# Attention on raw tokens, two taps per product, and smaller moves in a four-layer convolution and attention kernel

## The chip, the core and the metric

The kernel runs on one core of a Trainium2 chip. The metric is device microseconds of one execution; a time given for a kernel is the median of several. The profile comes from one further execution, taken by the hardware profiler. Its engines are PE (matrix multiplication, with PEld for its weight loads), DVE (vector), ACT (scalar), POOL (used here for fills alone) and SP, which issues the DMA transfers.

## The reference

A sequence of 2048 tokens with 512 features passes four layers, each with a residual. Layers 1 and 3 are a long convolution (a state-space kernel K of 128 modes per feature, multiplied with the input in a Fourier transform of length 4096; Kf and Uf below are the spectra); layers 2 and 4 are local attention with 32 heads of 16 features, in which a token looks at itself and at the seven tokens that lie 2, 4, ..., 14 before it. Both kinds get layer-normalized tokens, and the same weights serve both layers of a kind. In the code below q, k and v are the three parts of x @ wqkv, and kg and vg are k and v gathered at idx.

```python
def _layernorm(x, axis=-1, eps=1e-5):
    m = jnp.mean(x, axis=axis, keepdims=True)
    v = jnp.var(x, axis=axis, keepdims=True)
    return (x - m) / jnp.sqrt(v + eps)
...
def _A_ref(u, A_re, A_im, B_re, B_im, C_re, C_im, log_dt, Dskip):
    ...
    P = jnp.exp(logdA[:, :, None] * l[None, None, :])
    K = jnp.einsum("dn,dnl,dn->dl", Cc, P, dB).real
    ...
    Yf = Uf * Kf[None, :, :, :]
    ...
def _B_ref(x, wqkv, wo):
    ...
    idx = pos[:, None] - off[None, :]
    mask = idx >= 0
    ...
    logits = jnp.einsum("bhsd,bhswd->bhsw", q, kg) * scale
    logits = jnp.where(mask[None, None, :, :], logits, -1e9)
    attn = _softmax(logits, axis=-1)
    o = jnp.einsum("bhsw,bhswd->bhsd", attn, vg)
    return (lambda x, *d: x.transpose(*d))(o, 0, 2, 1, 3).reshape(B, S, D) @ wo

x = A_u
x = x + _A_ref(_layernorm(x, axis=-1), ...)
x = x + _B_ref(_layernorm(x, axis=-1), B_wqkv, B_wo)
x = x + _A_ref(_layernorm(x, axis=-1), ...)
x = x + _B_ref(_layernorm(x, axis=-1), B_wqkv, B_wo)
```

## The kernel before

The tokens `X` stay in on-chip memory as 128 partitions by 16 rows of 512 features; token p*16+j is row j of partition p. So a tap that lies 2w tokens back is row j-2w of the same partition, or of the partition before it, for which `shift` and a like transfer of kT copy the last rows one partition down.

Order. Each operation is registered with `Plan.op` with its engine, a planned duration in microseconds and what it needs; `Plan.either` registers several ways to do one step (on ACT or DVE, by PE or DMA). `Plan.run` then issues them in an order that is written out by hand in `ORDERS`, five strings of operation numbers, which also settles which way is taken. Each engine works through its share of that order, waiting where an input isn't there. The strings are in turn: preparation, kernel tables and first convolution, attention 1, convolution 2, attention 2.

Preparation and tables (`prepare`, `kernel_and_first_conv`). The convolution's kernel is built from tables of powers on DVE. Their factors, the multipliers A and B, come from casts on ACT (L556); A is stored twice side by side so that a factor meets pairs of elements. The table products (L391, L399, L456) are summed on PE (L431, L469).

Convolution. Spectra come from PE and are multiplied by the kernel's spectrum in two DVE products of 1024 elements each, `pa` and `pb` (L931, L932 in the first layer, L1176, L1177 in the second), which are joined with a sum and a difference, transformed back on PE, evacuated to `VT` (L959, L1205; its last index runs over 128 features), and brought into X by final matmuls (L981, L1222) and an evacuation (L985, L1227).

Attention (`b_layer`). It opens with 15 matmuls that nobody reads (L1271). For each quarter of four rows, `start` does statistics on DVE (L153; parts of them lie in the convolution's tail), a square root on ACT (L166), a reciprocal (L178), the normalization into `xn` (L193 on DVE, L1288 on ACT), and the transposes into `xnT`, by DMA (L1294) or PE (L1299). `proj` makes q and k (L1324, evacuated at L1329), `values` makes v (L1344, evacuated into `VX` at L1349). `logits` multiplies q with k for each of eight taps on DVE (L1375), 40 products a layer; PE sums the 16 features of a head with the 32-column matrix `bones` (L1385). The logits are copied, transposed and evacuated to `L` (L1400, L1408, L1411), the first partition's missing taps are filled by POOL (L1451), and a tree of maxima (L1430), a subtraction (L1473), Exp on ACT (L1474), a sum on PE (L1468), a reciprocal on DVE (L1456) and a multiplication (L1476) make the softmax. `pv` multiplies each tap's v with its weight on DVE (L1487) and PE sums the taps (L1503, L1508). The result is copied and turned (L1523, L1528) and multiplied by wo (`out`, L1560), and X is added by PE or DVE (L1543).

The attention's weights are loaded before the first convolution ends (L128 to L132, at 189.5 to 193 us).

Of the kernel before, what the change touches and what calls it, by code (L numbers as in the profile page):

```python
# [11 lines left out]
ALU = mybir.AluOpType  # L12
# [29 lines left out]
TWO_PI = 2.0 * np.pi  # L42

# [79 lines left out]
def load_b_weights(nc, const, wqkv, wo):  # L123
    wqk = const.tile([128, 4, 1024], BF, name="wqk")
    wo_t = const.tile([128, 4, 512], BF, name="wo_t")
    wv = const.tile([128, 4, 512], BF, name="wv")
    wsrc = wqkv.rearrange("(t p) f -> p t f", p=128)
    nc.sync.dma_start(wqk[:], wsrc[:, :, 0:1024])  # L128
    nc.sync.dma_start(wv[:], wsrc[:, :, 1024:1536])
    for ft in range(4):  # L130
        src = wo[ft * 128:(ft + 1) * 128, :].rearrange("(h d) o -> d h o", d=DH)
        nc.sync.dma_start(wo_t[:, ft, :], src)  # L132
    VX = const.tile([128, 2, NV + NJ, 256], BF, name="VX")
    nc.gpsimd.memset(VX[0:1, :, 0:NV], 0.0)
    return dict(wqk=wqk, wv=wv, wo=wo_t), VX


class LnStats:


    def __init__(self, nc, pool, parts, nm, eps, tag="", st=None):
        self.nc, self.parts, self.eps = nc, parts, eps
        p, t = st or (pool, "ln_st" + tag)
        self.st = p.tile([128, NJ, len(parts), 6], F32, name="ln_st_" + nm, tag=t)
        self.mv = pool.tile([128, NJ, 2], F32, name="ln_mv_" + nm, tag="ln_mv" + tag)
        self.den = pool.tile([128, NJ], BF, name="ln_den_" + nm, tag="ln_den" + tag)
        self.rstd = pool.tile([128, NJ], F32, name="ln_rstd_" + nm, tag="ln_rstd" + tag)
        self.nb = pool.tile([128, NJ], F32, name="ln_nb_" + nm, tag="ln_nb" + tag)
# [6 lines left out]
    def finish(self, j0, j1):  # L155
        self.gathered(j0, j1)
        self.root(j0, j1)
        self.scale(j0, j1)

# [12 lines left out]
    def root_of_squares(self, j0, j1):  # L172
        js = slice(j0, j1)
        self.nc.scalar.activation(self.den[:, js], self.sq[:, js], ACT.Sqrt, bias=self.eps[:, 0:1], scale=1.0 / D)

    def invert(self, j0, j1):
        js = slice(j0, j1)
        self.nc.vector.reciprocal(self.rstd[:, js], self.den[:, js])  # L178
# [4 lines left out]

    def scale(self, j0, j1):
        self.invert(j0, j1)
        self.offset(j0, j1)
# [9 lines left out]
def load_params(nc, pp, prm):  # L196
# [1533 lines left out]
```

## The time and profile before

| | |
|---|---|
| median of 3 runs | 498.18 us (497.74 to 498.95) |
| profiled execution, first to last instruction | 495.2 us; its own device time was not taken, the median lies 3.0 above the span |
| tables and first convolution | 0 to 204.9 us |
| attention 1 | 204.9 to 320.6 us (its last vector work ends at 325.65, beside convolution 2) |
| convolution 2 | 320.6 to 377.3 us |
| attention 2 | 377.3 to 495.2 us |
| busy | PE 411.3, DVE 457.7, ACT 349.0, POOL 13.0 us |
| granted clock of PE | 0.979 |

A stage here begins when the last part of X of the stage before is written. Times in the prediction's profile lines are microseconds from the span's start; a group's line gives the line of code, engine, operation, destination and sources, shapes, count, then busy time in all, mean nanoseconds of one, and the idle time before it with what ended it.

### The profile page before, as it was taken

To read this page: it belongs to the slowest core of one execution; us is meant where nothing else is said; L and a number is where in the kernel's file an instruction comes from. 1 tells how busy PE (TensorE), PEld (TensorE's weight loads), DVE (VectorE), ACT (ScalarE), POOL (GpSimd) and SP (SyncE) were. 2 spreads that over 40 slices of the span, in tenths; PEclk is the share of its full clock that TensorE was granted. 3 is DMA by queue.
4 is the path that set the end of the run, shared out by engine and by line. 5 is a ranking of instruction groups with operands and counts; after the bars stand their busy time and mean duration, and the time that the engine had idled before them with its cause. 6 is when DMAs were issued, how large, how long until landed. Compare 5 with 4: busy or idle time off the path is not lost.

```text
span 495.2 us, 12551 instructions
## 1 busy us (share of the span) xinstructions
PE 411.3 (83%) x5262; PEld 244.4 (49%) x5279; DVE 457.7 (92%) x774; ACT 349.0 (70%) x522; POOL 13.0 (3%) x63
## 2 busy tenths in 40 slices
PE   2602397988898989789999889979998999997996
PEld 1501262665575667543355434565675434563343
DVE  6999999999999998859899999988999689999996
ACT  6999986988778769764664359878997657643340
POOL 0000000000000004000000000000000000000000
PEclk9999698999999999999999989989999999999999
DMA  8930025448556846280031232559901500222217
GB/s 263 197 160 0 1 68 130 81 115 192 114 114 162 152 109 195 68 126 32 18 91 38 58 65 42 165 125 210 182 4 21 112 29 31 77 61 58 42 29 205
DMA packets 101596, 48.81 MB, mean 99 GB/s; under 512 B 86443, under 2 KB 93868, under 8 KB 101284
## 3 DMA queue, kind: packets, MB, share of 16 engines
q1 hardware_dynamic: 101108, 47.62, 41.6%
q8 instruction: 41, 0.67, 0.6%
q10 hardware_dynamic: 432, 0.39, 0.2%
q14 instruction: 15, 0.12, 0.1%
HBM read 15.78 MB, written 8.13 MB: 48 GB/s over the span
## 4 chain that ended last, share of the span: by engine, by line
PE 35%; DVE 12%; DMA 8%; ACT 7%; issue 5%; SPq 1%; POOL 0%; DVEq 0%; ACTq 0%
PE ps_qk L1324 7%; PE po L1503 4%; DVE prod L1487 4%; PE ps_v L1344 4%; PE ps_o L1560 3%; DVE prod L1375 3%; DMA VX<-VX 2%; PE Lp L1385 2%; DMA zt<-Z 2%; PE ps_y L1222 1%; PE vp L1196 1%; PE vp L1200 1%; DMA xnT<-xn 1%; ACT L L1474 1%; ACT Z L845 1%
## 5 line engine op out<-in xcount | busy, mean ns | idle before, releaser
L1375 DVE TENSOR_TENSOR prod<-qT,kT 128x2048 bf16<-128x2048 bf16 (+1 forms) x80 | 76.9, 1006 | 12.6 <-ACT kT L1329 9.9
L1487 DVE TENSOR_TENSOR prod<-VX,L 128x2048 bf16<-128x2048 bf16 (+2 forms) x96 | 77.3, 862 | 1.3 <-DMA VX<-VX 1.0
L1324 PE MATMUL ps_qk<-xnT,wqk 128*128 128x512 bf16 x256 | 61.4, 380 | 1.5 <-DMA xnT<-xn 1.3
L1503 PE MATMUL po<-prod,sb_ident 128*128 128x512 bf16 x216 | 53.5, 379 | 4.8 <-DVE prod L1487 3.7
L1324 PEld LDWEIGHTS <-wqk 128*128 128x128 bf16 x256 | 22.8, 97 | 31.9 <-issue 9.7
L1503 PEld LDWEIGHTS <-sb_ident 128*128 128x128 bf16 x224 | 21.2, 98 | 31.3 <-DVE prod L1487 5.1
L1344 PE MATMUL ps_v<-wv,xnT 128*128 128x256 bf16 x256 | 32.1, 273 | 1.9 <-ACT xnT L1302 1.4
L431 PE MATMUL ps_sum<-Ttab,sb_ident 128*128 128x512 bf16 x36 | 15.1, 420 | 22.2 <-DVE Ttab L391 21.4
L1349 ACT CAST VX<-ps_v 128x512 bf16<-128x512 f32 x32 | 18.6, 587 | 19.8 <-PE ps_v L1344 19.7
L845 ACT CAST Z<-ps_s 128x1024 bf16<-128x1024 f32 (+1 forms) x32 | 29.4, 983 | 3.4 <-PE ps_s L840 2.4
L1560 PE MATMUL ps_o<-wo_t,oT 128*128 128x512 bf16 x108 | 29.4, 388 | 0.6 <-DVE X L1543 0.2
L1329 ACT CAST qT<-ps_qk 128x512 bf16<-128x512 f32 x31 | 17.9, 587 | 16.8 <-PE ps_qk L1324 16.7
L1344 PEld LDWEIGHTS <-xnT 128*128 128x128 bf16 x256 | 24.1, 98 | 10.0 <-issue 3.4
L1523 ACT CAST ot<-po 128x1024 bf16<-128x1024 f32 x14 | 13.8, 1014 | 21.4 <-PE po L1503 21.4
L1385 PE MATMUL Lp<-prod,sb_bones 128*32 128x512 bf16 x256 | 25.6, 390 | 3.6 <-DVE prod L1375 3.6
L456 DVE TENSOR_TENSOR Ttab<-Ttab,MPA 128x2048 bf16<-128x2048 bf16 (+2 forms) x20 | 28.4, 1434 | 0.1
L456 DVE TENSOR_TENSOR Y2tab<-Ttab,MPB 128x6144 bf16<-128x6144 bf16 (+1 forms) x13 | 27.3, 2123 | 0.6 <-PE psk L472 0.6
L1329 ACT CAST kT<-ps_qk 128x512 bf16<-128x512 f32 x32 | 18.7, 586 | 10.9 <-PE ps_qk L1324 10.7
L840 PEld LDWEIGHTS <-sb_F 128*128 128x128 bf16 x256 | 16.1, 103 | 18.3 <-issue 15.7
L153 DVE BATCH_NORM_STATS2 ln_st_b<-X 128x6 f32<-128x128 bf16 (+2 forms) x80 | 23.0, 358 | 0.3 <-ACT X L985 0.3
L436 ACT CAST Ttab<-ps_sum 128x1024 bf16<-128x1024 f32 (+1 forms) x20 | 18.3, 940 | 6.0 <-PE ps_sum L432 4.6
L469 PE MATMUL psk<-Ttab 128*32 128x64 bf16 x1024 | 21.5, 199 | 1.1 <-DVE Ttab L456 0.9
(228 smaller groups left out, 1035.2 us busy)
## 6 DMA issues: line engine op xcount, KB each, us to landing
X<-in_A_u_dram SPq DMA_DIRECT2D x8, 512.0 KB, 5.4
kt_scratch<-sp_k SPq DMA_DIRECT2D x16, 256.0 KB, 3.3
Kt<-kt_scratch SPq DMA_DIRECT2D x16, 256.0 KB, 5.0
k_scratch<-KTq SPq DMA_DIRECT2D x7, 256.0 KB, 2.6
KT<-k_scratch SPq DMA_DIRECT2D x7, 256.0 KB, 3.7
VX<-VX SPq DMA_DIRECT2D x4, 448.0 KB, 4.4
kT<-kT SPq DMA_DIRECT2D x8, 192.0 KB, 2.2
out_dram<-X SPq DMA_DIRECT2D x3, 512.0 KB, 3.6
```

Source lines behind the costliest of these rows:

```text
L153: self.nc.vector.bn_stats(self.st[:, j, part, :], X[:, j, a:b])
L456: nc.vector.tensor_tensor(d, src.to_broadcast([128, c, n, 2 * EYB]), mm.to_broadcast([128, c * n, EYB, 2]), ALU.mult)
L469: nc.tensor.matmul(o.rearrange("e (s i) -> e s i", s=2), xs, T[:, 1:3, h, m // 2, :, t], start=(m == 0), stop=False, skip_group_check=True)
L845: nc.scalar.copy(box["Z", kind, dc][:, 0:n // 8, :, jq * 32:(jq + 1) * 32].rearrange("p g r k -> p r g k"), box.pop(("s1", kind, dc, jq))[ ...
L1324: nc.tensor.matmul(ps[:], wqk[:, ct, f0:f0 + 128], xnT[:, 4 * s:4 * s + 4, ct, :], start=(ct == 0), stop=(ct == 3))
L1329: copy((qT, kT)[which][fp][:, f2, o:o + 512], box.pop(("qk", which, fp, f2, s))[:])
L1344: nc.tensor.matmul(ps[:, jj].rearrange("p t h d -> p (t h d)"), xnT[:, j + jj, ct, :], wv[:, ct, fp * 256:(fp + 1) * 256], start=(ct == 0) ...
L1375: nc.vector.tensor_tensor(pr[:, 0:n2], qT[fp][:, a:a + n2, j0 * 128:j0 * 128 + 1024], kT[fp][:, a:a + n2, c0:c0 + 1024], ALU.mult)
L1385: nc.tensor.matmul(Lp[r0:r0 + 32, w // 4, :], bones[:, w % 4, :], pr[:, f2 - a, hb * 512:(hb + 1) * 512], start=(n == 1), stop=(n == 4), s ...
L1487: nc.vector.tensor_tensor(p2[:, 0:nj].rearrange("p j t d h -> p (j t) d h"), VX[:, fp, NV + a:NV + a + nj].rearrange("p j (t d h) -> p (j ...
L1503: nc.tensor.matmul(po[:, c:c + 512], ident[:], p2[:, k + j:k + j + 2].rearrange("p j t d h -> p (j t d h)"), start=(n == 1), stop=(n == W))
L1560: nc.tensor.matmul(ps, box["oT"][:, ft // 2, j, ft % 2, :], wo_t[:, ft, :], start=(ft == 0 and not res), stop=(ft == 3))
```

## The change

- Layer norm in attention: the tokens are no longer normalized. X itself is transposed into U (now the input of proj and values, named XT). The mean is taken out of the weights once, in attention 1: every column of wqkv loses its mean over the 512 inputs. The reciprocal deviation of a token comes from column sums of U on PE, 16 Square operations with accumulation on ACT, then Ln and Exp(-0.5 x). v is scaled by it when it is evacuated (two operations of 256 columns in place of one of 512), and logits are multiplied by the product of the query's and the key's (`RR`, four DVE multiplications of 1024 elements a layer).
- Two taps per DVE product: logits from 40 to 20 products a layer (twice as long), weights times v from 48 to 36. L is laid out by tap.
- Softmax: the reciprocal may be Ln and Exp(-x) on ACT. All square roots become Ln and Exp, and one function table that has both is loaded once.
- Multipliers A are stored once and spread when read.
- The two products with the spectrum become one DVE instruction of 2048 elements.
- VT is laid out in eight pieces of 16 features, and the final matmuls read it at a stride.
- The attention's weight loads move into attention 1's order on SP. The last two rows of `out` use accumulators of their own.
- All five orders are new. Counted from them, the changes between 32-column and full-width matmuls go from 50 to 34 in the first convolution, 44 to 16 in attention 1 and 48 to 20 in attention 2.

The core of the diff (orders and much else left out):

```diff
-        self.nc.scalar.activation(self.den[:, js], self.mv[:, js, 1], ACT.Sqrt, bias=self.eps[:, 0:1])
+        self.nc.scalar.activation(self.den[:, js], self.mv[:, js, 1], ACT.Ln, bias=self.eps[:, 0:1])
+        self.nc.scalar.activation(self.rstd[:, js], self.den[:, js], ACT.Exp, scale=-0.5)
...
-        self.base = [pool.tile([128, n, 8, 2, HD, 2, 2], BF, name="MU" + x) for x, n in (("A", 3), ("B", 4))]
+        self.base = [pool.tile([128, n, 8, 2, HD, c, 2], BF, name="MU" + x) for x, n, c in (("A", 3, 1), ("B", 4, 2))]
...
-                nc.vector.tensor_tensor(pa[:], x[:], k[:, 0:1, :].to_broadcast([128, 2, 512]), ALU.mult)
-                nc.vector.tensor_tensor(pb[:], x[:], k[:, 1:2, :].to_broadcast([128, 2, 512]), ALU.mult)
+                nc.vector.tensor_tensor(pr[:], x[:].unsqueeze(1).to_broadcast([128, 2, 2, 512]),
+                                        k[:].unsqueeze(2).to_broadcast([128, 2, 2, 512]), ALU.mult)
...
-                    box["VT", dc] = one.tile([128, 2, NJ, DCH], BF, name="VT", tag="VT")
+                    box["VT", dc] = one.tile([128, 8, 2, NJ, 16], BF, name="VT", tag="VT")
...
+        def windows(a, step, n):
+            return bass.AP(a.tensor, a.offset, [list(a.ap[0]), [step, n], *[list(z) for z in a.ap[1:]]])
...
+            def mean():
+                ps = box["wm", name] = psA.tile([128, 512], F32, name="ps_wm", tag="psA")
+                for ct in range(4):
+                    nc.tensor.matmul(ps[:], mones[:], w[:, ct, sl], start=(ct == 0), stop=(ct == 3))
+            def add():
+                ps = box.pop(("wm", name))
+                nc.vector.tensor_tensor(w[:, :, sl], w[:, :, sl], ps[:].unsqueeze(1).to_broadcast([128, 4, 512]), ALU.add)
...
+            def sums():
+                ps = box["sum", q] = psA.tile([128, 4], F32, name="ps_sum", tag="psA")
+                for j in range(j0, j1):
+                    for ct in range(4):
+                        nc.tensor.matmul(ps[:, j - j0:j - j0 + 1], XT[:, j, ct * 128:ct * 128 + 128], mones[:, 0:1],
+                                         start=(ct == 0), stop=(ct == 3), skip_group_check=True)
+            def square(j):
+                nc.scalar.activation(oT[:, j // 8, j % 8 * D:j % 8 * D + D], X[:, j, :], ACT.Square, bias=nm[:, j:j + 1], accum_out=rs[:, NV + j:NV + j + 1])
...
+                for jj in range(2):
+                    scaled(VX[:, fp, NV + j + jj].rearrange("p (t d h) -> p t d h", t=2, d=DH),
+                           ps[:, jj].rearrange("p t h d -> p t d h"), rs[:, NV + j + jj:NV + j + jj + 1])
...
-                    nc.vector.tensor_tensor(pr[:, 0:n2], qT[fp][:, a:a + n2, j0 * 128:j0 * 128 + 1024],
-                                            kT[fp][:, a:a + n2, c0:c0 + 1024], ALU.mult)
+                    nc.vector.tensor_tensor(pr[:], windows(q, 0, 2),
+                                            windows(kT[fp][:, a:a + n2, col(w):col(w) + 1024], -DIL * 128, 2), ALU.mult)
...
+            def scaled():
+                Lj = L[fp][:, j0 // 8].rearrange("p w j t h -> p (w j) t h")
+                nc.vector.tensor_tensor(Lj, Lj, RR[:, j0 // 8].rearrange("p w j h -> p (w j) h").unsqueeze(2)
+                                        .to_broadcast([128, W * 8, 2, 8]), ALU.mult)
...
+                    nc.vector.tensor_tensor(p2[:].rearrange("p w j t d h -> p w (j t) d h"), windows(v, -DIL * 256, taps),
+                                            l.to_broadcast([128, taps, nj * 2, DH, 8]), ALU.mult)
```

More of the change, by code (lines that the diff above doesn't have):

```diff
@@ L126, in load_b_weights @@
     wv = const.tile([128, 4, 512], BF, name="wv")
+    mones = const.tile([128, 128], BF, name="mones")
+    VX = const.tile([128, 2, NV + NJ, 256], BF, name="VX")
     wsrc = wqkv.rearrange("(t p) f -> p t f", p=128)
[L128 to L135, printed above, removed]
+    return dict(bones=bones, wqk=wqk, wv=wv, wo=wo_t, mones=mones, qksrc=wsrc[:, :, 0:1024], vsrc=wsrc[:, :, 1024:1536],
+                osrc=[wo[ft * 128:(ft + 1) * 128, :].rearrange("(h d) o -> d h o", d=DH) for ft in range(4)]), VX
 class LnStats:
@@ L358, in __init__, with spread @@
         self.T, self.Y2 = {}, {}
+    @staticmethod
+    def spread(m, e):
+        n, c = m.shape[1:3]
+        return m.rearrange("p n c t -> p (n c) t").unsqueeze(2).to_broadcast([128, n * c, 2 // c * e, 2])
     def ones(self, hc):
@@ L1091, in kernel_and_first_conv, with a_layer @@
             pl.run()
-    return X, ln_b, C["last"]
-def a_layer(nc, tc, C, X, kt_dram, U, ln_b):
+    return X
+def a_layer(nc, tc, C, X, kt_dram, U):
     with ExitStack() as es:
@@ new lines, in centred, with by_vector, by_tensor, mm @@
+        def centred(name, w, c0):
+            sl, loaded = slice(c0, c0 + 512), [Wl["wv" if name == "v" else "wqk"], Wl["mones"]]
+            def mean():
[5 more added lines that the diff above has]
+                nc.vector.tensor_tensor(w[:, :, sl], w[:, :, sl], ps[:].unsqueeze(1).to_broadcast([128, 4, 512]), ALU.add)
+            def by_vector():
+                key = ("psA", "wm", name)
+                a = pl.op("P", 0.87, mean, loaded, take=key)
+                return pl.op("V", 2.2, add, a, drop=key)
+            def by_tensor():
+                ps, out = [], []
+                for h in range(2):
+                    def mm(h=h):
+                        ps = box["wc", name, h] = psO.tile([128, 2, 512], F32, name="ps_wc", tag="psO")
+                        for k in range(2):
+                            nc.tensor.matmul(ps[:, k], ident[:], w[:, h * 2 + k, sl], start=True, stop=False)
+                            for ct in range(4):
+                                nc.tensor.matmul(ps[:, k], mones[:], w[:, ct, sl], start=False, stop=(ct == 3))
+                    ps.append(pl.op("P", 2.16, mm, loaded, take=("psO", "wc", name, h)))
+                for h in range(2):
+                    out.append(pl.op("A", 0.92, lambda h=h: nc.scalar.copy(w[:, h * 2:h * 2 + 2, sl], box.pop(("wc", name, h))[:]), ps,
+                                     drop=("psO", "wc", name, h)))
+                return out
+            Wd[name] = pl.either(("wc", name), by_vector, by_tensor)
@@ L1301, in evac @@
-            def evac(j2):
-                nc.scalar.copy(xnT[:, j2 * 2:j2 * 2 + 2].rearrange("c j t p -> c (j t p)"),
-                               box.pop(("x", j2))[:].rearrange("c k p -> c (k p)"))
-            a = pl.op("V", 1.12, stats, pl.outer(("x", q)))
-            a = pl.op("A", 0.2, lambda: ln_b.root(j0, j1), a)
-            a = pl.op("V", 0.12, lambda: ln_b.invert(j0, j1), a)
-            a = pl.op("V", 0.09, lambda: ln_b.offset(j0, j1), a)
-            ns = [norm(j) for j in range(j0, j1)]
@@ new lines, in start, with by_pe, by_dma @@
+            ready = [pl.outer(("xe", q)), pl.outer(("x", q))]
+            def by_pe():
+                out = []
+                for cp in range(2):
+                    b = pl.op("P", 0.5, lambda cp=cp: turn_mm(cp), ready[cp], take=("psO", "x", q, cp))
+                    out.append(pl.op("A", 0.92, lambda cp=cp: turn_evac(cp), b, drop=("psO", "x", q, cp)))
+                return out
+            def by_dma():
+                return [pl.op("S", 1.4, lambda j=j: turn_dma(j), ready, lag=3.2) for j in (j0, j0 + 2)]
@@ new lines, in square, with root @@
+            def square(j):
+                nc.scalar.activation(oT[:, j // 8, j % 8 * D:j % 8 * D + D], X[:, j, :], ACT.Square, bias=nm[:, j:j + 1], accum_out=rs[:, NV + j:NV + j + 1])
+            def root():
+                r = rs[:, NV + j0:NV + j1]
+                nc.scalar.activation(nm[:, js], r, ACT.Ln, bias=eps[:, 0:1], scale=1.0 / D)
+                nc.scalar.activation(r, nm[:, js], ACT.Exp, scale=-0.5)
+            key = ("psA", "sum", q)
+            a = pl.op("P", 0.9, sums, turned[q], Wl.get("mones", []), take=key)
@@ new lines, in start, with pairs, shifted, spread @@
+            a = pl.op("V", 0.1, lambda: nc.vector.tensor_copy(nm[:, js], box.pop(("sum", q))[:]), a, drop=key)
+            a = [pl.op("A", 0.72, lambda j=j: square(j), a) for j in range(j0, j1)]
+            Rs[q] = pl.op("A", 0.5, root, a)
+        def pairs():
+            def shifted():
+                nc.sync.dma_start(rs[1:128, 0:NV], rs[0:127, NV + NJ - NV:NV + NJ])
+            def spread():
+                for jh in range(2):
+                    nc.scalar.copy(RR[:, jh], rr[:, jh * 8:jh * 8 + 8].rearrange("p j w -> p w j").unsqueeze(3)
+                                   .to_broadcast([128, W, 8, 8]))
+            def ones():
+                for w in range(1, W):
+                    for j0 in range(0, DIL * w, 8):
+                        nc.gpsimd.memset(RR[0:1, j0 // 8, w, 0:min(8, DIL * w - j0), :], 1.0)
+            o = pl.op("G", 0.1, lambda: nc.gpsimd.memset(rs[0:1, 0:NV], 1.0))
+            o = pl.op("S", 0.5, shifted, o, *Rs.values(), lag=2.3)
+            o = pl.op("V", 0.2, lambda: nc.vector.tensor_tensor(rr[:], rs[:, NV:].unsqueeze(2).to_broadcast([128, NJ, W]),
+                                                                back(rs[:, NV:]), ALU.mult), o)
+            o = pl.op("A", 0.92, spread, o)
+            box["RR"] = pl.op("G", 0.8, ones, o)
@@ L1318, in proj, with back @@
+        def back(a):
+            return bass.AP(a.tensor, a.offset, [list(a.ap[0]), list(a.ap[1]), [-DIL, W]])
         def proj(which, fp, f2, s):
@@ new lines, in inverted, with log, power @@
+            def inverted(act, us, src, a, drop):
+                if act:
+                    def log():
+                        box["ln", fp, j0] = small.tile([128, 128], F32, name="sm_ln", tag="sm_s")
+                        nc.scalar.activation(box["ln", fp, j0][:], src(), ACT.Ln)
+                    def power():
+                        box["rdb", fp, j0] = small.tile([128, 128], BF, name="sm_rdb", tag="sm_rdb")
+                        nc.scalar.activation(box["rdb", fp, j0][:], box.pop(("ln", fp, j0))[:], ACT.Exp, scale=-1.0)
+                    a = pl.op("A", 0.3, log, a, take=("sm_s", "ln", fp, j0), drop=drop)
+                    return pl.op("A", 0.3, power, a, take=("rdb", fp, j0), drop=("sm_s", "ln", fp, j0))
+                return pl.op("V", 0.87 * n / 8, lambda: invert(src()), a, take=("rdb", fp, j0), drop=drop)
@@ new lines, in sums @@
+                    for t in range(taps):
+                        first, stop = n == 1 and t == 0, n == W // taps and t == taps - 1
+                        for k in range(0, nj, np):
+                            po = box["po", fp, j0 + k]
+                            for j in range(0, np, 2):
+                                c = j * 256
+                                if flat:
+                                    nc.tensor.matmul(po[:, c:c + 512], ident[:],
+                                                     p2[:, t, k + j:k + j + 2].rearrange("p j t d h -> p (j t d h)"),
+                                                     start=first, stop=stop)
+                                    continue
+                                for x in range(4):
+                                    nc.tensor.matmul(po[:, c + x * 128:c + x * 128 + 128],
+                                                     p2[:, t, k + j + x // 2, x % 2].rearrange("p d h -> p (d h)"),
+                                                     ident[:], start=(first and x == 0), stop=stop, skip_group_check=True)
@@ L1511, in part @@
                 key = ("prod", "v", fp, j0, w)
-                o = pl.op("V", vt(nj * 256), prod, Sd[fp, j0 // 8 * 8], [Vd[fp, j] for j in range(a, a + nj)], *box.get("pv", []), take=[key])
+                o = pl.op("V", vt(nj * taps * 256), prod, Sd[fp, j0 // 8 * 8], [Vd[fp, j] for j in range(a - DIL * (taps - 1), a + nj)], *box.get("pv", []), take=[key])
                 vs.append(o)
-                return pl.op("P", (0.115 if flat else 0.14) * nj, sums, o, *([] if first is None else [first]), drop=key,
+                return pl.op("P", (0.115 if flat else 0.14) * nj * taps, sums, o, *([] if first is None else [first]), drop=key,
```

352 lines of the change are left out of this document (159 added, 193 removed), and 123 rows, old and new, of the table ORDERS.

## The prediction

> **What bounds the kernel now.** First the page's opening, for the engines' totals.
>
> ```profile
> span 495.2 us, 12551 instructions
> PE 411.3 (83%) x5262; PEld 244.4 (49%) x5279; DVE 457.7 (92%) x774; ACT 349.0 (70%) x522; POOL 13.0 (3%) x63
> ```
>
> DVE is busy 92% of the span, PE 83%. That is a mean over four stages, so next come the busy windows by stage: tables and first convolution, attention 1, convolution 2, attention 2. Columns: window, length, then busy PE, PEld, DVE, ACT, POOL, clock, DMA share, GB/s.
>
> ```profile
> 0.00:204.00 204.00, 143.99 (x3363) 99.60 (x3365) 194.10 (x294) 170.91 (x236) 8.24 (x23) 0.97 0.54 129
> 204.00:320.60 116.60, 107.65 (x716) 54.30 (x722) 105.70 (x190) 71.47 (x125) 2.40 (x20) 0.99 0.28 64
> 320.60:377.00 56.40, 52.04 (x488) 37.85 (x486) 52.38 (x110) 50.91 (x81) 0.00 (x0) 0.97 0.58 122
> 377.00:495.20 118.20, 107.62 (x701) 52.64 (x708) 105.52 (x183) 55.75 (x84) 2.40 (x20) 1.00 0.29 69
> ```
>
> Only the first stage is DVE's alone (194 of 204, PE 144). In both attentions PE is as full as DVE (107.65 beside 105.70, 107.62 beside 105.52), and in convolution 2 three engines are above 90%. So DVE time saved there is worth less than its size.
>
> Each attention has two phases, split at DVE's first logits product (220.06 and 391.00):
>
> ```profile
> 204.97:220.06 15.09, 13.03 (x78) 6.92 (x79) 8.96 (x45) 10.29 (x18) 0.00 (x0) 1.00 0.67 106
> 377.30:391.00 13.70, 12.90 (x74) 6.65 (x75) 10.11 (x54) 9.00 (x16) 0.00 (x0) 1.00 0.53 99
> 220.06:325.65 105.59, 96.95 (x656) 48.72 (x662) 100.55 (x157) 64.43 (x112) 2.40 (x20) 0.98 0.25 68
> 391.00:492.10 101.10, 94.72 (x628) 45.99 (x633) 95.10 (x128) 46.46 (x67) 2.40 (x20) 1.00 0.25 63
> ```
>
> Before the product PE ends last; after it DVE leads PE by 3.6 and 0.4 us. The chain of waits names what stands in series:
>
> ```profile
> 203.63 0.87 DVE ln_st_b L153 x4
> ...
> 210.48 5.18 DMA xnT<-xn
> 215.79 3.61 PE ps_qk L1324 x16
> ...
> 241.32 1.28 ACT L1474
> ...
> 412.62 1.28 ACT L1474
> 413.92 1.06 ACT L L1474
> ```
>
> Statistics, normalization, transposes and projections open the attention one after another; twice the chain holds a load of ACT's function table ahead of Exp.
>
> Last the groups by shape (busy, mean ns of one) for prices:
>
> ```profile
> L1375 DVE TENSOR_TENSOR prod<-qT,kT 128x2048 bf16<-128x2048 bf16 x48 | 56.6, 1218 | 1.7 <-ACT qT L1329 0.6 <-ACT kT L1329 0.6 <-DMA kT<-kT 0.5
> L456 DVE TENSOR_TENSOR Ttab<-Ttab,MPA 128x4096 bf16<-128x4096 bf16 x7 | 16.0, 2289 | 0.1
> L399 DVE TENSOR_TENSOR Ttab<-Ttab 128x2048 bf16<-128x2048 bf16 x4 | 4.9, 1224 | 0.1
> ```
>
> and three pieces of PE's timeline (start, us), for the price of a visit to another tile shape:
>
> ```profile
> 248.98 0.60 PE L1344 MATMUL ps_v<-wv,xnT 128*128 128x256 bf16 x4
> 249.51 0.40 PE L1385 MATMUL Lp<-prod,sb_bones 128*32 128x512 bf16 x4
> 249.85 0.61 PE L1344 MATMUL ps_v<-wv,xnT 128*128 128x256 bf16 x4
> ```
>
> A product of 4096 costs 2289 ns against 2×1218, so merging two saves about 0.15 us of duration; issued back to back their starts lie 1.14 and 2.20 us apart, which saves 0.08.
>
> **The change part by part.** Per engine I add the durations that the code plans for each operation, along the old and the new order. These sums agree with the windows within 4 us in attention (109.3 planned, 105.7 traced for DVE in attention 1), so I use their differences. 0.3% (1.5 us) is about what a measurement can tell from no change. The span is 495.2; the median of the runs is 498.18, so 3.0 lies outside it, and I keep that.
>
> *Tables and first convolution.* Up to the last table operation DVE's sum is 117.1 before, 117.7 after: storing multipliers once takes casts from ACT, which is hidden by DVE, and saves nothing. Uncovered it would be ACT's 5 us (50.6 to 45.5). In the tail, DVE loses 8.9 us of statistics, which were filler there, gains 4.2 in joins and evacuations, and merges its product pairs; ACT goes 19.8 to 17.0, PE 21.7 to 23.1. The orders have 16 fewer changes between 32-column and full-width matmuls. In the solid stretches 512-column matmuls start every 0.217 us, 256-column ones every 0.109. So four of these end at 249.41, the sums (L1385, four tiles at once) start 0.10 later and hold PE for 0.34 instead of 0.22: a visit costs 0.22, and two changes make one, −1.8. Between −3 and +1.4 (PE's growth, nothing returned) I take **−1.5**.
>
> *Attention 1, before the first product.* Gone: statistics, root, norm, and transposes' wait on them; raw transposes can start as each quarter of X lands. Added on PE after the idle matmuls: q and k means, 2×4 matmuls of 512 columns at 0.217 us, 1.74 together; two groups of 10 for v, 2×2.17; column sums of 16 one-column matmuls, 0.9 a quarter. In the new order two means, both v groups, two groups of sums and eight projections stand before the product: idle 3.25 + 1.74 + 4.34 + 1.74 + 8×0.87 + 1.0 for evacuation = 19.0 after the last X, against 15.1: **+3.9**. DVE's two weight additions, 2.2 each, lie beside this (DVE was idle 6.1 of 15.1); with that cover gone they would cost up to 4.4. What is queued behind them are q and k evacuations. The weight DMAs move from 189.5 to behind SP's last spectrum stores (197.21 and 1.33 long); they took 5.3 us to land, 204 to 206, under the idle matmuls. If they land late it is at most 2 us.
>
> *Attention 1, after it.* DVE 99.8 to 96.6: 32 products fewer (20 logits, 12 values) at 0.08 is −2.6, reciprocals of 951 ns move to ACT, four multiplications of 1024 elements at 0.61 are added. PE 96.5 to 97.3, but 28 tile changes fewer: 14×0.22 = −3.1, net −2.3. Both must fall for the end to fall, so I take −2.3 to −3.2, middle −2.8. The table load on the chain goes, −1.3. ACT rises 63.3 to 81.1 in 116.6, and V's evacuation now waits for 16 squarings: hidden while ACT has 35 us of slack, but values' products queue behind it. With +3.9 this gives **−0.2**, between −3 and +4.
>
> By the Trainium skill ("ScalarE: Activation LUTs", What ACT_TABLE_LOAD costs) a switch is 1283 ns of load and 1380 ns of drain. Here the load starts at 412.62 and Exp at 413.92, so the drain doesn't show. By that rule both loads together would give 5.3 and not 2.6, and the whole forecast 489.1.
>
> *Convolution 2.* DVE loses 8.2 us of statistics at 369.39 to 377.6, again filler after its own last products; 1.2 goes with merged products (16×0.08). ACT 46.5 to 42.7, PE 49.2 to 48.3. PE is at 40.74 of 42 from 335 to 377, so what PE loses counts: −0.9, with merges partly: **−1.7**, between 0 and −4. The final matmuls read pieces of 16 columns at a stride. No row shows that; contiguous 128-column ones last 0.24 (L1119), 0.054 apart by the spacing of the wider ones. I take 0, the row's rate, since they cannot beat it; at half the rate 128 of them would cost 128×0.054 = 7 more in each convolution, the term I can bound worst.
>
> *Attention 2.* No centring. Sums 0.9 a quarter replace the wait on norm, first product **+1.4** (two groups of sums less one group of transposes, 2×0.95 − 0.5). After it DVE 93.6 to 92.6, PE 94.5 to 95.9 less 14 visits fewer (−3.1), so −1.0 to −1.7, middle −1.4; table load −1.3. Work that DVE did before the product (10.1 to 4.0) frees its queue for evacuations: a further −1.7, between 0 and −3, where DVE is full (35.00 of 35 from 430 to 465). Together **−3.0**.
>
> Sum: −1.5 −0.2 −1.7 −3.0 = −6.4, so 495.2 − 6.4 + 3.0 = 491.8.
>
> **The rivals.**
> *All of DVE's cut counts.* DVE's planned total goes 451.1 to 431.2, with merges 428.8. At constant idle (37.5) that is −22, 476. For: 92% busy, full from 100 to 204. Against: 17 us of it is statistics in places where DVE had nothing else, and PE's fill in attention.
> *Attention becomes PE-bound, slower.* Place: start of attention 1 and 2. Raw tokens put 6.1 of centring and 7 of sums ahead of projections; the +3.9 and +1.4 stay, DVE returns nothing because PE paces it, and the planned PE growth after the product (0.8 and 1.4) adds without the tile visits' return: 7.5, less the −1.5 of the first stage: 504. It decides once the visits' 0.22 is a hidden gap and not PE time. For: PE at 44.72 of 46 from 384 to 430. Against: DVE leads after 220.06.
> *No change.* New work fills what normalization left, within 1.5 of 498.2. For: the small net of attention 1.
> *Two taps do not run at the rate of one.* The windows overlap and step backwards between taps. If the rate halved, most of the products' present 76.9 + 77.3 us (L1375, L1487) would come again, some 120, and the time would pass 600. Against: L399 reads with a step backwards at 1224 ns, as fast as 1218. The change does what it says if these rows read 2.29.
>
> **How the numbers follow.** Forecast −3 to −12: 0.52, because two phases of four carry a measured excess. DVE's whole cut: 0.18. PE-bound: 0.21, for the price of a visit rests on one group. No change: 0.08. Two taps slow: 0.01. Hence faster 0.70, same 0.08, slower 0.22. The forecast's own range is 486 to 495. The time goes to 478 below (most of the DVE rival) and to 503 above, just short of the PE rival: attention 1's +4, no gain in the convolutions and part of the strided reads' cost.
>
> **What would show it.** Right: two-tap rows at about 2.29 us; the first product 18 to 20 us after the last X in attention 1; no table load ahead of Exp; conv 2 shorter by 1 to 2 with no statistics at its end; tables ending at about the same time as before. Wrong: DVE idle growing beyond 40 us with PE solid in attention (the second rival), or final matmuls longer than 0.24.

## The result and the profile after

The changed kernel takes 492.37 us (median of 4 runs, 489.57 to 493.79), beside 498.01 for the kernel before in the same comparison: a ratio of 0.988, 95% interval 0.984 to 0.9919. That is 5.6 us less; forecast were 6.4 less and 491.8. The profiled execution took 491.45, with a span of 489.3, 5.9 below the span before.

The page's opening, after:

```profile
span 489.3 us, 12680 instructions
PE 408.0 (83%) x5400; PEld 249.0 (51%) x5400; DVE 434.8 (89%) x549; ACT 359.1 (73%) x618; POOL 15.1 (3%) x86
```

DVE's busy time fell by 22.9 us, 225 instructions, and the span by 5.9: a quarter of it. PE is busy 3.3 us less, ACT 10.1 more. Where the rest went is read from the busy windows, cut at the last table product, the last part of X of a layer, and the first logits product of each attention (columns as in the prediction):

```profile
0.00:176.18 176.18, 116.33 (x2962) 81.04 (x2963) 170.14 (x225) 144.87 (x198) 2.23 (x23) 1.00 0.57 122
176.18:202.58 26.40, 23.41 (x398) 18.05 (x396) 17.18 (x25) 18.83 (x28) 6.21 (x2) 1.00 0.57 164
202.58:220.70 18.12, 18.06 (x112) 8.57 (x113) 6.89 (x8) 8.73 (x20) 0.00 (x0) 1.00 0.68 118
220.70:321.30 100.60, 95.95 (x691) 50.80 (x690) 96.77 (x116) 76.27 (x169) 3.31 (x30) 0.98 0.23 55
321.30:374.54 53.24, 48.36 (x472) 35.17 (x472) 45.89 (x70) 46.62 (x75) 0.10 (x1) 1.00 0.73 153
374.54:388.35 13.81, 13.51 (x103) 6.60 (x103) 4.64 (x9) 8.31 (x21) 0.00 (x0) 1.00 0.65 129
388.35:489.30 100.95, 92.33 (x667) 48.78 (x665) 93.30 (x98) 55.49 (x113) 3.28 (x30) 1.00 0.23 64
```

In the tail of the first convolution DVE went from 23.57 busy to 17.18 and the tail stayed as long (26.6, 26.4): those were fillers. In both openings (third and sixth line) PE is now busy throughout, 18.06 of 18.12 and 13.51 of 13.81. Convolution 2 lost 4.8 us of DVE (50.67 to 45.89) and 1.2 of length.

The same cuts in the kernel before are 178.30, 204.92, 220.06, 322.80, 377.28 and 390.97 us (the cut at 320.6 that stands ahead of the prediction lies 2.2 before attention 1's last part of X). The last column gives the span of the same stretch in the changed kernel and those of the experiments below that changed nothing in it; it is the scatter against which an edit is read. Of the kernel before there is one trace, so its own scatter is not known.

| stretch | before | after | change | forecast | unedited runs |
|---|---|---|---|---|---|
| to the last table product | 178.3 | 176.2 | −2.1 | 0 | 175.4 to 177.9, mean 176.5 |
| tail of the first convolution | 26.6 | 26.4 | −0.2 | −1.5 | 25.3 to 27.5 |
| attention 1 to its first product | 15.1 | 18.1 | +3.0 | +3.9 | 18.1 |
| attention 1, the rest | 102.7 | 100.6 | −2.1 | −4.1 | 99.3 to 100.6, mean 99.7 |
| convolution 2 | 54.5 | 53.2 | −1.2 | −1.7 | 52.6 to 54.2, once 56.1 |
| attention 2 to its first product | 13.7 | 13.8 | +0.1 | +1.4 | 13.8 |
| attention 2, the rest | 104.2 | 101.0 | −3.3 | −4.4 | 100.8 to 101.2, mean 101.0 |

Part of this scatter has a cause that the traces show. PE's granted clock falls to half for 3.41 us, or a whole number of times 3.41, at places that differ from trace to trace. In attention 1 behind its first product, DVE's operations in the changed kernel and in two_products (below) start at the same times, counted from that product, to 0.01 us, up to 290 us. But the clock of the changed kernel was at half from 287.0 to 290.4, and at the end it lies 1.3 us behind. Where the clock stayed full, this stretch took 99.3 us (99.28 to 99.32 in four traces with the same orders). The one trace of the kernel before was at half there too, from 288.0 to 291.4, so the −2.1 compares like with like. In convolution 2 it was at half from 325.6 to 329.0, and the changed kernel was not.

The chain of waits shows no table load any more. Three groups by shape settle what no row of before showed (busy, mean ns):

```profile
L1434 DVE TENSOR_TENSOR prod<-qT,kT 128x4096 bf16<-128x4096 bf16 x24 | 53.9, 2290 | 1.6 <-ACT kT L1374 0.8 <-ACT rs L1332 0.5 <-ACT qT L1374 0.3
L1573 DVE TENSOR_TENSOR prod<-VX,L 128x4096 bf16<-128x4096 bf16 x24 | 53.9, 2291 | 0.1
L1189 PE MATMUL ps_y<-VT,sb_F1T 128*128 128x128 bf16 x128 | 9.8, 219 | 0.8 <-DVE VT L1172 0.8
```

Two taps in one instruction cost 2290 ns, as a plain product of that size (2289), though the windows overlap and step backwards. The final matmuls last 219 ns with strided reads, and lasted 219 before.

### The profile page after: what moved, and what is told of

It is laid out like the page before. It is cut to its first block, busy times and chain, and to the rows that moved or that the text cites. A ratio compares the mean times of both kernels' runs of the same rounds, so it can differ in the third digit from the quotient of the medians.

```text
span 489.3 us, 12680 instructions
## 1 busy us (share of the span) xinstructions
PE 408.0 (83%) x5400; PEld 249.0 (51%) x5400; DVE 434.8 (89%) x549; ACT 359.1 (73%) x618; POOL 15.1 (3%) x86
## 5 line engine op out<-in xcount | busy, mean ns | idle before, releaser
L1573 DVE TENSOR_TENSOR prod<-VX,L 128x512 bf16<-128x512 bf16 (+2 forms) x72 | 75.6, 1103 | 1.0 <-PE po L1589 0.6
L1434 DVE TENSOR_TENSOR prod<-qT,kT 128x4096 bf16<-128x4096 bf16 (+1 forms) x40 | 72.5, 1863 | 1.8 <-ACT kT L1374 0.8
L1369 PE MATMUL ps_qk<-U,wqk 128*128 128x512 bf16 x256 | 58.7, 379 | 0.4 <-ACT L L1476 0.2
L1400 ACT ACTIVATE VX<-ps_v,rs 128x256 bf16<-128x256 f32 x64 | 26.5, 473 | 8.1 <-PE ps_v L1389 7.6
L1327 ACT ACTIVATE oT<-X,nm 128x512 bf16<-128x512 bf16 x32 | 22.8, 714 | 12.9 <-DVE nm L1335 12.7
L1389 PE MATMUL ps_v<-wv,U 128*128 128x256 bf16 x256 | 31.3, 272 | 0.7 <-ACT VX L1400 0.3
L1389 PEld LDWEIGHTS <-U 128*128 128x128 bf16 x256 | 24.6, 98 | 7.6 <-issue 2.0
L1607 ACT CAST ot<-po 128x1024 bf16<-128x1024 f32 x14 | 13.8, 1011 | 17.7 <-PE po L1589 17.7
L458 PE MATMUL psk<-Y2tab,Ttab 128*32 128x48 bf16 x1024 | 21.0, 193 | 5.3 <-issue 3.6
L907 DVE TENSOR_TENSOR pa<-sp_u,sp_k 128x2048 bf16<-128x2048 bf16 x16 | 19.3, 1221 | 3.8 <-PE vp L931 2.6
L379 DVE TENSOR_TENSOR Ttab<-Ttab,MUB 128x256 bf16<-128x256 bf16 (+4 forms) x36 | 22.5, 626 | 0.0
```

Of the source, the lines that this page charges most:

```text
L379: nc.vector.tensor_tensor(self.spare(hc, False)[:, x0:x1, :, :, 0:m, :].rearrange("n x h c e t -> n (x h c) e t"), src, mult(1), ALU.mult)
L1327: nc.scalar.activation(oT[:, j // 8, j % 8 * D:j % 8 * D + D], X[:, j, :], ACT.Square, bias=nm[:, j:j + 1], accum_out=rs[:, NV + j:NV + j ...
L1369: nc.tensor.matmul(ps[:], wqk[:, ct, f0:f0 + 128], XT[:, 4 * s:4 * s + 4, ct * 128:ct * 128 + 128], start=(ct == 0), stop=(ct == 3))
L1389: nc.tensor.matmul(ps[:, jj].rearrange("p t h d -> p (t h d)"), XT[:, j + jj, ct * 128:ct * 128 + 128], wv[:, ct, fp * 256:(fp + 1) * 256] ...
L1400: nc.scalar.activation(out, ps, ACT.Identity, scale=r)
L1434: nc.vector.tensor_tensor(pr[:], windows(q, 0, 2), windows(kT[fp][:, a:a + n2, col(w):col(w) + 1024], -DIL * 128, 2), ALU.mult)
```

## The experiments

All are edits of the changed kernel and are compared with it: 492.37 us, and the table above.

**The opening of the attentions.** First, without the unread matmuls (no_idle):

```diff
-        for _ in range(15):
+        for _ in range(0):
             nc.tensor.matmul(idle[:], ident[:], ...)
```

> The changed kernel without the 15 matmuls that nobody reads at the start of each attention. Theory A (on raw tokens PE paces the opening, so these matmuls, once hidden behind normalization and transposes, now stand in the path): the first logits product comes 15 x 0.217 = 3.2 us sooner after the last X in each attention (18.1 to 14.9, 13.9 to 10.6), and the kernel takes about 486 instead of 492.4. Rival B (the DMA transposes pace the opening as before): the product moves by at most 1 us, the time by 0 to 2. Rival C (PE's granted clock falls after the pause): matmul spacing above 0.217 and a time of 492 or more.

Measured: 490.38 us (ratio to before 0.9846, 0.9797 to 0.9895; not told apart from the changed kernel's). The first product came 18.13 and 13.81 us after the last X, as with them. So 3.25 us of matmuls were removed from a PE that had no pause, and neither opening became shorter. The windows show why, first of the kernel without them, in steps of 3.41 us, and then of the changed kernel over much the same work:

```profile
203.53:206.94 3.41, 1.18 (x10) 0.48 (x11) 0.63 (x1) 0.00 (x0) 0.00 (x0) 1.00 1.04 193
206.94:210.35 3.41, 3.41 (x24) 1.44 (x22) 2.35 (x2) 2.65 (x7) 0.00 (x0) 0.50 1.00 187
374.20:377.61 3.41, 1.59 (x27) 0.99 (x25) 1.79 (x4) 0.38 (x1) 0.00 (x0) 1.00 0.83 155
377.61:381.02 3.41, 3.41 (x9) 1.21 (x8) 1.38 (x2) 1.84 (x6) 0.00 (x0) 0.50 0.99 187
```

```profile
206.00:211.00 5.00, 5.00 (x39) 2.45 (x37) 2.98 (x3) 2.93 (x8) 0.00 (x0) 1.00 1.03 193
377.80:383.00 5.20, 5.20 (x49) 2.63 (x48) 2.24 (x4) 3.68 (x10) 0.00 (x0) 1.00 1.02 190
```

In attention 1 PE paused 0.8 us and, for the transposes of U, 1.5 us; in attention 2 it paused 1.8 us. In the step behind these pauses its granted clock was 0.50, where the unread matmuls hold 1.00: four matmuls of 512 columns came to 1.91 us where they take 1.03. In attention 1 the pause for transposes (1.50) and the slower stretch up to the second column sums (7.57 us instead of 6.03) give 3.04 of the 3.25 back, so theories B and C hold together, each for half, though the time of 492 or more that C named did not come. In attention 2 PE kept 1.1 us of its lead, and then the product itself waited for another transfer, kT's copy one partition down, which SP issued at 385.7, when ACT had evacuated kT:

```profile
389.64 2.36 DVE L1433 TENSOR_TENSOR prod<-qT,kT 128x2048 bf16<-128x2048 bf16 x2 [1.15 <-DMA kT<-kT]
```

The Trainium skill ("TensorE: Matmul & The Clock Gate", HAM oscillation) says that PE falls back to half rate when it waits for a DMA long enough to cross a monitoring window, which it puts at 3.4 us. The traces agree in the half rate and in the 3.4 us, but much less waiting was enough. In the fourteen traces of this case, cut into steps of 3.41 us as their records of the clock are, each of the 51 falls to half follows a step in which PE stood idle for 1.61 us or more. None of the 1703 steps at full clock that no fall followed had more than 1.86 us of it. So it is idle time of about half a step, in one pause or in several, that came ahead of each fall.

Second, without the centring (no_centring):

```diff
             def mean():
-                ps = box["wm", name] = psA.tile([128, 512], F32, name="ps_wm", tag="psA")
-                for ct in range(4):
-                    nc.tensor.matmul(ps[:], mones[:], w[:, ct, sl], ...)
+                pass
...
```

> The changed kernel without the centring of the weights (its matmuls, additions and copies are left out, so the mean stays in q, k and v). Theory A (PE paces the opening): 28 matmuls fewer, the first product 6.1 us sooner, 18.1 to 12.0 after the last X, and attention 1 as a whole shorter by the same 6, the kernel at about 486. Rival B (DVE paces what follows, so an early start is partly given back): the product 6 sooner but attention 1 only 2 to 4 shorter, 488 to 490. Rival C (transposes pace it): the product at most 3 sooner.

Measured: 494.13 us (0.9917, 0.9887 to 0.9947). The first product came 17.18 us after the last X, 0.94 sooner and not 6.1, so theory A falls and C holds: PE waited 1.61 and 1.48 us for transposes of U, and its clock was at half between these waits, from 209.8 to 213.2. The time is not below the changed kernel's; its convolution 2 took 56.1 us, the one value outside the others; PE's clock was at half there from 332.7 to 336.1, and why it fell this edit does not explain. Two bounds lie close together in this opening, PE's sum of work (18.1) and the row of transposes with the clock that their pauses cost (17.2 with none of the centring). Here the 6.1 us of centring cost about 1.

Third, centring first, in the place of the unread matmuls (centre_first; `center` is true in attention 1):

```diff
-"2 84 0 12 3 4 57 56 62 63 21 41 1 6 13 7 66 42 123 20 ..."
+"2 84 0 12 3 4 57 56 41 1 6 13 7 21 20 62 63 66 42 123 ..."
-        for _ in range(15):
+        for _ in range(0 if center else 8):
```

> The changed kernel with an order of PE in attention 1 that does all centring first, in the place of the 15 matmuls that nobody reads, and 8 of those instead of 15 in attention 2. Theory: the transposes pace the opening, and the unread matmuls are there only so that PE does not pause, after which its clock would fall; work that is needed does that as well. The first product comes 3 us sooner in attention 1 (18.1 to 15.0) and 1.5 sooner in attention 2 (13.8 to 12.3), the clock stays at 1.0, and the kernel takes 4 us less, about 488.5. Rival: PE still pauses for a transpose, the clock falls as without those matmuls, and the time is 491 to 493.

Measured: 489.55 us (0.982, 0.9795 to 0.9845), 2.8 less than the changed kernel and the fastest of all, though the two intervals touch. The first product came after 16.71 and 13.16 us instead of 18.12 and 13.81, a gain of 1.4 and 0.65 where 3 and 1.5 were expected; the clock stayed at 1.00. In attention 2 the product waited 0.83 us for kT's copy. What was left over in attention 1 is a pause of PE, here in its timeline:

```profile
210.80 1.02 PE L1315 MATMUL ps_qk<-U,wqk 128*128 128x512 bf16 x4 [0.25 <-DVE nm L1281]
213.05 10.70 PE L1315 MATMUL ps_qk<-U,wqk 128*128 128x512 bf16 x48 [1.23 <-ACT qT L1320]
```

The projection waited for an accumulator that ACT had to evacuate, and ACT was doing four squarings first. Both pauses lie in one step of 3.41 us, 1.48 in all, and no fall of the clock followed.

Fourth, on top of it, a quarter transposed by PE (one_quarter_by_pe):

```diff
-"... 20 62 63 66 42 123 ... 31 76 75 30 ..."
+"... 20 22 23 62 63 42 123 47 48 26 28 27 29 ... 76 75 ..."
```

> The kernel with centring first, in which also the transposes of one of the four quarters are done by PE (16 of them, 0.9 us, and two ACT copies of 1.0) instead of two DMA transposes. If the row of DMA transposes on SP paces the opening (PE there paused 1.2 us between 211.8 and 213.05): the pause goes, the first product comes 0.3 to 1 us sooner than the 16.7 us after the last X, the kernel at about 489. If PE's sum of work paces it, it comes 0.9 later, 490.5; either way between the two-queue version's 489.55 and 1 us off it.

Measured: 493.29 us (0.991, 0.9881 to 0.9939), the first product after 21.26 us (489.55 is the time with centring first). Both theories missed. The first took the pause at 213.05 to be a wait for transposes; the line above names ACT, which neither theory counted. The two copies of transposes put 1.93 us more on ACT ahead of the squarings and evacuations, PE paused 1.01 and 2.26 us for evacuations, and its clock was at half from 217.6 to 221.1.

**The price of a change of tile.** By itself (visits):

```diff
         wide(15)
+        if center:
+            narrow(12)
+            wide(24)
+        else:
+            for _ in range(12):
+                narrow(1)
+                wide(2)
```

> The changed kernel with more matmuls that nobody reads at the start of each attention, to price a change of tile: after the 15 wide ones, attention 1 gets 12 groups of four 32-column matmuls and then 24 wide ones, attention 2 the same 12 groups and 24 wide ones in turns (one group, two wide). If a visit to the 32-column tiles costs 0.22 us of PE, as the forecast took it, the second stretch lasts 11 x 0.22 = 2.4 us longer than the first (about 10.2 against 7.8). If the changes cost nothing, both last the same; at 0.1 the difference is 1.1.

The windows of the grouped stretch (12 groups of four 32-column matmuls, then 24 wide ones) and of 11 turns of the alternating one:

```profile
205.81:213.71 7.90, 7.90 (x74) 3.55 (x74) 0.00 (x0) 0.00 (x0) 0.00 (x0) 1.00 1.14 166
385.20:394.74 9.54, 9.54 (x68) 2.37 (x68) 0.00 (x0) 0.00 (x0) 0.00 (x0) 1.00 0.59 111
```

A turn takes 9.54 / 11 = 0.867 us; its three matmul times of 0.217 make 0.65. A visit costs 0.22, as the one group of the prediction gave it. The Trainium skill ("TensorEngine Tiling (Array Packing)", Key Properties) says that a change of tiling mode drains PE and gives no price; this is one. In its place (visits_back):

```diff
+                        if k == 0 and n2 == 2:
+                            nc.tensor.matmul(Lp[:, w // 4, 0:1], ident[:], zero[:, 0:1], start=False, ...)
```

> The changed kernel with one full-width matmul of a single column of zeros between the two taps' groups of 32-column sums, in the 12 two-tap sums of each attention that cover both halves: 24 changes of tile more in each attention, nearly the 28 that the change took out. If a visit's price counts in full: 12 x 0.22 = 2.6 us in each attention, 5.3 in all, 497.5. If half of it falls where PE waits for DVE anyway: 1.3 in each, 495. If PE has room there: under 0.5 in each.

Measured: 491.89 us (0.9879, 0.985 to 0.9908), no slower. PE did pay: the sums on either side of an added matmul start 0.42 us apart, and 0.21 without it. But the rest of attention 1 took 100.0 and that of attention 2 101.8 us, with the clock full. That is 0.7 and 0.9 above the traces without the edit whose clock was full too (99.3 and 100.95), where 2.6 each was the full price. The places where this was put back are logits phases, in which DVE has the next product going anyway; the places where the kernel before had its visits were not tried.

**The two taps** (one_tap):

```diff
-                    nc.vector.tensor_tensor(pr[:], windows(q, 0, 2), windows(kT[fp][...], -DIL * 128, 2), ALU.mult)
+                    for k in range(2):
+                        nc.vector.tensor_tensor(pr[:, k], q, kT[fp][:, a:a + n2, col(w + k):col(w + k) + 1024], ALU.mult)
...
```

> The changed kernel with each two-tap product issued as two instructions of one tap each: 64 more DVE instructions at 0.08 us, 32 in each attention. If DVE paces attention after its first product: 2.6 us more in each attention, 497.5 in all. By the forecast's accounting (DVE and PE pace in turns): 1 to 2 more in each, 494.5 to 496.5. If PE paces it: under 0.5 in each, 492 to 493.

Measured: 492.18 us (0.9881, 0.9841 to 0.9922), no difference. The rest of attention 1 took 100.6 and that of attention 2 101.7, 1.3 and 0.7 above the same full-clock traces. So two taps are worth some 2.0 us. DVE's busy time grew by 3.7 for the 64 instructions (434.8 to 438.5), where 5.1 had been priced, so about half of it counts; in the whole time that is lost in the scatter.

**The table loads.** A first try (table_load):

```diff
+                nc.scalar.activation(root2[:], eps[:], ACT.Sqrt)
```

> The changed kernel with one square root of a single column on ACT after the spread of the deviations in each attention, so that ACT must load its function table again before the next Exp, as in the kernel before. By the forecast: 1.3 us more in each attention, 2.6 in all, 495. By the rule of the Trainium skill with a drain behind each load: 5.3. Rival (ACT's wait is covered by work that PE and DVE have queued): 0 to 0.5 in all, 492.4 to 493.

Measured: 532.01 us (1.067, 1.0633 to 1.0707), far above every expectation. Once the square root has displaced the table that has both Ln and Exp, the program gets a load at every turn from one to the other: 38 more loads, 48.8 us of ACT. As a single load it says nothing; as a price it says that the kernel grew by some 40 us for 48.8 of loads. So the second (table_wait) puts the joint table back itself:

```diff
+                if "root" not in box:
+                    box["root"] = 1
+                    nc.scalar.activation(root2[:], Lf[:, 0, 0:1], ACT.Sqrt, bias=eps[:, 0:1], scale=0.0)
+                    nc.scalar.preload_act_table_set(LN_EXP)
                 nc.scalar.activation(Lf, Lf, ACT.Exp, scale=DH ** -0.5)
```

> The changed kernel with two loads of ACT's function table ahead of the first Exp of each attention (a square root of a single column of the logits, which waits for them as Exp does, and then the table with Exp): two loads and a short operation, 2.8 us on ACT in front of Exp, against one load of 1.3 in the kernel before. If all of a load there counts, as in the forecast: 2.8 in each attention, 5.6 in all, 498; half: 2.8 in all; if products are queued beside it: under 1 in all.

Measured: 497.66 us (1.0006, 0.9981 to 1.0031), 5.3 more: all that the change had brought. The rest of attention 1 took 102.0 and of attention 2 104.1 us, 2.7 and 3.1 above the full-clock traces, for 2.9 us on ACT in each:

```profile
418.19 1.28 ACT L1521 ACT_TABLE_LOAD   x1
419.49 0.29 ACT L1521 ACTIVATE root<-L,eps 128x1 f32<-128x1 bf16 x1
419.80 1.28 ACT L1522 ACT_TABLE_LOAD   x1
```

In attention 1, with the clock full, ACT time right ahead of Exp counts at nine tenths. A likely reason is that DVE and PE hold nothing else for that pair of heads; that is not shown by itself. In attention 2 PE paused 3.1 us and its clock was at half from 422.1 to 425.6, so a part of the 3.1 there may be the clock's. After each load the next operation starts 1.30 us behind the load's start (419.49 and 421.10). The drain of 1380 ns that the Trainium skill adds to a load ("ScalarE: Activation LUTs", What ACT_TABLE_LOAD costs) does not appear here either.

**Three edits that were costed at little or nothing.** Two spectrum products (two_products):

```diff
+                for i in range(2):
+                    nc.vector.tensor_tensor(pr[:, i], x[:], k[:, i:i + 1, :].to_broadcast([128, 2, 512]), ALU.mult)
```

> The changed kernel with the product of a token's and the kernel's spectrum issued as two DVE instructions of 1024 elements again, in both convolutions: 16 more instructions in each at 0.08 us. By the forecast (merging counts partly): 0.5 to 1.2 more in convolution 2 and up to 1 in the tail of the first, 493 to 494.5. If PE and ACT pace both: under 0.5 in all.

Measured: 490.21 us (0.9845, 0.9809 to 0.9881); tail 25.1, convolution 2 53.5, neither longer than in the scatter above. VT by rows (vt_rows):

```diff
-                    box["VT", dc] = one.tile([128, 8, 2, NJ, 16], BF, name="VT", tag="VT")
+                    box["VT", dc] = one.tile([128, 2, NJ, DCH], BF, name="VT", tag="VT")
...
```

> The changed kernel with VT laid out by rows of 128 features again, so that evacuations write pieces of 16 at a stride and the final matmuls read at none. By the forecast the matmuls cost the same either way, 0.22 us as shown. If evacuations into pieces are slower when strided (651 ns of 512 columns in convolution 2 before), ACT gets up to 2 us in each convolution back and the kernel takes 492 to 495; if strided reads cost PE, the final matmuls get shorter and the kernel takes under 492.

Measured: 491.29 us (0.9861, 0.9824 to 0.9898), tail 27.5, convolution 2 53.9: no difference either. Multipliers A stored twice (a_twice):

```diff
-            return lambda: nc.scalar.copy(ma[:, :, :, c, :], src(0))
+            return lambda: [nc.scalar.copy(ma[:, :, :, k, :], src(0)) for k in range(ma.shape[3])]
...
```

> The changed kernel with multipliers A stored twice again, by a second copy behind the first. By the forecast ACT's copies are hidden by DVE: tables end at the same time, within the scatter that these runs show (175.4 to 177.9 us). Rival: the earlier end of the tables (176.2 after, 178.3 before) came from the fewer copies; then it is about 2 us later, 178 or more, and the kernel takes 494 to 495.

Measured: 493.6 us (0.9928, 0.9904 to 0.9951), tables to 178.9 us, 1.1 beyond the latest of the twelve other traces that share this code and 2.4 beyond their mean. DVE's waits show two that the changed kernel did not have, for ACT:

```profile
DVE lad L588 <- ACT sq L576: 1.4, 3, 0.7
DVE Ttab L393 <- ACT Ttab L422: 1.2, 1, 1.2
```

The copies are not hidden by DVE: they stand in ACT's queue ahead of squarings and table copies for which DVE waits.

## Why the prediction was right, and where its steps were not

The time, the sign and the size held (491.8 against 492.37), and so did the main reading: DVE's saving counts for a quarter, because most of it was filler or lay beside a PE that was as full. Of the rivals, all of DVE's cut (476), the slow one (504) and no change (498.2) fell; two taps run at full rate. But the sum was better than its terms, and that is luck: the seven rows of the table miss by 0.5 to 2.1 us each, some 9 in all, and the misses cancel to 0.6. One sign that the prediction had named as wrong did come: DVE is idle for 54.5 us, beyond 40. But the forecast itself implied some 53 (37.5, and 22 less work in a span 6.4 shorter), so that sign could not tell it from the slow rival.

*Tables, forecast 0.* The ladder's copies were taken to be covered by DVE. They were not: a_twice moves the tables' end by 2.4, about what the change had moved it. The end also scatters by 2.5 us in traces that share this code. Three of the twelve had their clock at half near 126 us and end at 177.6 to 177.9, the others at 175.4 to 177.0. The kernel before and a_twice had no fall there and still end later than all twelve, at 178.3 and 178.9. There is one trace of each, so how much of the 2.1 is the copies' stays open.

*Tail, forecast −1.5.* It moved by 0.2. That the statistics were filler was right; the joins, visits and merged products that were to count did not.

*Attention 1 before the product, +3.9.* The list of PE's work was right and the mis-sized term is the column sums: 16 one-column matmuls last 0.41 us, not 0.87, which is the 0.9 missing. The cause is deeper than the sum, though: take the 6.1 us of centring away and the transposes and the clock take their place. In attention 2 the same term explains most of +1.4 against +0.1.

*After the products, −4.1 and −4.4.* Measured were −2.1 and −3.3. The table load was right in size: nine tenths of it counts by table_wait, about 1.2 a layer. The visits were priced right (0.22) and placed wrong: where they were put back they lie beside DVE's products, and 24 of them cost 1.6 in both layers together, where the forecast took 28 of them, 6.2 us, off PE. The two taps give 2.0. These add to some 5.9, beside the 5.4 of the two rows, so nothing is left for the further 1.7 that DVE's freed queue was to bring in attention 2; no run tried that term by itself.

*Convolution 2, −1.7.* It is 1.2 shorter, within a scatter of 1.6, and of the two traces only that of before had its clock at half here, for 3.4 us. So no gain is shown. The statistics at its end were filler, as said, and the merged products are worth nothing that two_products shows.

## What to carry over

Price an edit twice: what its instruction costs, and who was waiting at that place. Less than a third of the price of the visits to another tile shape reached the time, and about half of what the single-tap products cost DVE, while ACT's time ahead of an Exp counted nearly in full. Compare a stretch of two traces only where their clocks are alike: one fall to half cost 1.3 us of attention 1, as much as the taps did there. Where two bounds lie close, as PE's work and the transposes in the opening, taking one away shows only the other; useful work that keeps PE going in the place of filler matmuls brought the two first products 2.1 us sooner here.

## What was not expected of the hardware

PE's granted clock fell to half, for 3.41 us at a time, behind steps of 3.41 us with 1.6 to 1.9 us of idle time or more, whether in one pause (1.8 us) or in two (0.8 and 1.5 us). So removing 15 matmuls that nobody reads shortened neither opening. And one square root between Ln and Exp of a joint table brought 38 more loads.
